# Seven block products for the down projection of a SwiGLU block, and gate and up products that stay in one PSUM bank

## The chip, the cores and the metric

The kernel runs on one core of one Trainium2 chip. The metric is the device time of one execution in microseconds (us), lower is better. One execution of the kernel before was also recorded by the hardware profiler, and all rows below come from that record.

## The reference

A transformer block in float32 on 2048 tokens of width 576: a modulated layer norm, attention with 32 heads in four segments, a residual, a second modulated layer norm, a SwiGLU feed-forward layer with 4608 hidden units, and a residual. The change is in the feed-forward layer alone:

```
x = x + ga * attention(h)                       # x: 2048 x 576
h = layernorm(x) * (1 + cb) + sb
g = silu(h @ w_gate)                            # w_gate, w_up: 576 x 4608
u = h @ w_up
x = x + gb * ((g * u) @ w_down)                 # w_down: 4608 x 576
```

## The kernel before, in words

The attention part fills the first third of the span and stays as it is, but for one transfer. The feed-forward layer then works on two halves of the tokens (`t` = 0, 1; 1024 tokens each), and in each half on 18 pairs of hidden blocks (`p`; 2 x 128 hidden units each). One pass of the inner body for one `t` and one `p` is called a step here; there are 36.

**Numbers as a high and a low part.** Every operand of a matmul is split into two reduced float32 values. For weights, ScalarE writes the high part `wh` (L1065), VectorE subtracts it and writes the low part `wl` (L1066), and GpSimd writes a small tail of `wh` (L1067). The hidden activation gets `ah` (ScalarE, L1110) and `al` (VectorE, L1111), the down weights `dh` (L1079) and `dl` (L1080). A product is high times high, low times high and high times low.

**Gate and up: seven block products.** Tokens, width and hidden units are each cut in two, which would make eight block products; the kernel makes seven (Strassen's scheme in Winograd's form) from sums of blocks. A step has 14 slots (`k`): seven products `m`, in the order `MO7`, for the gate (`z` = 0) and seven for the up weights (`z` = 1). Slot `k` runs `prod` (L1090): seven matmuls of 512 columns into one PSUM bank. The sums of weight blocks are GpSimd's (`sum_o`, L1059), those of token blocks `y` are made ahead. What the seven products mean for the four result blocks is worked out after them: VectorE adds the banks into `tx` and `ty` (L1122, L1125, L1129) and makes the four results (L1101 for the gate, which ScalarE then puts through silu at L1102; L1106 and the multiply by the gate at L1107 for the up part).

**Down: all block products.** `down` (L1152) makes, for one tile of 128 tokens, 12 matmuls of 288 columns into two banks, which VectorE adds to the running result `acc` in SBUF (L1155). Eight tiles make a step's down projection. They run one step late, at slots 4 to 11 of the next step. The down weights are loaded in `load_d`, multiplied there by `gb` on GpSimd (L1073), and split by `prep_d`. `acc` begins as the residual, so that after the last step each tile is stored as it is (L1158).

**Order.** The kernel is scheduled by hand: each engine gets its instructions in the order in which the Python code issues them, and runs them in that order. What the list `later` holds is issued at the start of the next slot. In each slot the order is: the weight split for the product seven slots ahead, the held-back subtractions, the product and its VectorE work, `sum_o`, the tile of `down`, the preparation of the down weights, and, for `t` = 0 alone, one piece of `prep2`, which makes the token blocks of the second half (`xD` to `yD`).

## Time and profile before

| | us |
|---|---|
| median of 3 runs | 1943.85 |
| lowest, highest | 1943.43, 1947.84 |
| span of the profiled execution, first to last instruction | 1946.8 |

| engine | busy us in the span | share |
|---|---|---|
| PE (TensorE matmuls) | 1901.2 | 98% |
| DVE (VectorE) | 1533.1 | 79% |
| POOL (GpSimd) | 1020.6 | 52% |
| ACT (ScalarE) | 824.8 | 42% |

The record gives the span and not the time outside it; the span is 2.9 us above the median of the runs and inside their scatter. The shares are averages over the attention and the feed-forward part. A busy PE is not the same as a PE that could not be faster, but where it is busy without a gap, and nothing waits ahead of it, the count of matmuls and the time of one set the pace.

### The profile page before, as it was taken

Reading aid. Unit: us, or ns where it says so; the run is one execution under the profiler, and the core shown is the slowest. Engines: PE = TensorE matmul, PEld = TensorE weight load, DVE = VectorE, ACT = ScalarE, POOL = GpSimd, SP = SyncE. Lnnn points to the kernel's source line nnn. Section 1 sums busy time; section 2 is a strip of 40 time slices with the busy share of each in tenths; the row PEclk is TensorE's granted clock in tenths of the full one; section 3 lists DMA queues with packets and bytes.
Section 4 is the critical chain, followed back from the end, with each engine's and each line's share of the span. In section 5 each row is a group of like instructions: output and inputs, shape, how many; then the busy total and the mean of one; then the engine's idle time right before and its main releaser. Section 6 shows DMA issues by size and latency. Waiting matters only on the chain.

```text
span 1946.8 us, 31901 instructions
## 1 busy us (share of the span) xinstructions
PE 1901.2 (98%) x11119; PEld 1593.1 (82%) x11119; DVE 1533.1 (79%) x3218; ACT 824.8 (42%) x1652; POOL 1020.6 (52%) x1396
## 2 busy tenths in 40 slices
PE   7999999999999899999999999999999999999999
PEld 4887865676766678888888888888888888888888
DVE  6575257878786999898898988979888888878886
ACT  2222256767667434344344343433333333333332
POOL 5322235455544866556565565556565564655551
PEclk9999999999999899999999999999999999999999
DMA  7776564444443332232222222174211211112111
GB/s 207 244 227 233 203 204 140 131 139 150 136 128 125 92 135 101 89 106 80 80 106 83 82 84 78 60 264 146 74 62 45 74 62 59 60 62 74 62 57 50
DMA packets 114354, 223.59 MB, mean 115 GB/s; under 512 B 22992, under 2 KB 40784, under 8 KB 112720
## 3 DMA queue, kind: packets, MB, share of 16 engines
q1 hardware_dynamic: 111936, 215.61, 34.2%
q0 software_dynamic: 576, 5.11, 0.7%
q8 instruction: 88, 1.44, 0.3%
q10 hardware_dynamic: 1680, 0.82, 0.2%
q14 instruction: 74, 0.61, 0.1%
HBM read 161.11 MB, written 60.36 MB: 114 GB/s over the span
## 4 chain that ended last, share of the span: by engine, by line
PE 88%; DVE 4%; DMA 4%; ACT 1%; issue 1%; POOL 1%; SPq 1%; POOLq 0%; ACTq 0%; DVEq 0%
PE M L1090 39%; PE pd L1152 23%; PE pp L93 4%; PE s L576 4%; PE av L596 4%; PE s L174 4%; PE pv L93 3%; PE pw L694 2%; DMA O<-in_wgu_dram 1%; DMA mD<-mr 1%; PE pn L765 1%; PE pm L429 1%; PE px L617 1%; PE pr L346 1%; DVE y L923 1%
## 5 line engine op out<-in xcount | busy, mean ns | idle before, releaser
L1090 PE MATMUL M<-y,wh 128*128 128x512 f32 x2520 | 792.0, 393 | 5.0 <-DVE cu L1106 2.1
L1090 PEld LDWEIGHTS M<-y,wh 128*128 128x128 f32 x2520 | 473.7, 188 | 101.7 <-issue 3.9
L1067 POOL TENSOR_TENSOR wh<-O,wh 32x128 fp32r<-32x128 f32 x504 | 296.6, 593 | 423.0 <-ACT wh L1065 271.3
L1090 PE MATMUL M<-y,wl 128*128 128x512 f32 x1008 | 394.7, 392 | 0.0
L1059 POOL TENSOR_TENSOR O<-O 128x384 f32<-128x384 f32 x288 | 315.4, 1095 | 75.0 <-DMA O<-in_wgu_dram 42.9
L1152 PE MATMUL pd<-dh,ah 128*128 128x288 f32 x1152 | 340.3, 295 | 0.2 <-DVE acc L1155 0.2
L1152 PE MATMUL pd<-dl,ah 128*128 128x288 f32 x1152 | 340.3, 295 | 0.0
L1152 PE MATMUL pd<-dh,al 128*128 128x288 f32 x1152 | 340.1, 295 | 0.0
L1110 ACT CAST ah<-sg 128x512 fp32r<-128x512 f32 x144 | 89.5, 621 | 547.8 <-DVE sg L1107 422.0
L1155 DVE TENSOR_TENSOR acc<-acc,pd 128x576 f32<-128x576 f32 x288 | 216.5, 752 | 111.8 <-PE pd L1152 108.4
L1066 DVE TENSOR_TENSOR wl<-O,wh 128x256 fp32r<-128x256 f32 x504 | 286.2, 568 | 6.0 <-ACT wh L1065 5.2
L179 DVE CUSTOM_DVE_ANT_0 junk<-s,tri 128x256 bf16<-128x256 f32 (+3 forms) x512 | 228.7, 487 | 77.2 <-PE s L174 69.8
L1065 ACT CAST wh<-O 128x384 fp32r<-128x384 f32 x504 | 242.8, 507 | 0.0
L1152 PEld LDWEIGHTS pd<-dl,ah 128*128 128x128 f32 x1152 | 217.4, 189 | 11.8
L1152 PEld LDWEIGHTS pd<-dh,ah 128*128 128x128 f32 x1152 | 216.7, 188 | 11.6 <-DVE acc L1155 0.6
L579 ACT ACTIVATE Pt<-s 128x512 f32<-128x512 f32 (+1 forms) x352 | 186.5, 559 | 88.1 <-PE s L576 72.0
L1152 PEld LDWEIGHTS pd<-dh,al 128*128 128x128 f32 x1152 | 216.6, 188 | 0.0
L1090 PEld LDWEIGHTS M<-y,wl 128*128 128x128 f32 x1008 | 190.0, 188 | 29.6
L1102 ACT ACTIVATE sg<-sg 128x512 f32<-128x512 f32 x144 | 91.2, 633 | 222.7 <-DVE sg L1101 222.7
L576 PE MATMUL s<-qs,ks 110*128 110x512 f32 (+2 forms) x384 | 150.5, 409 | 5.7 <-DMA qs<-mD 4.4
L174 PE MATMUL s<-ks,qs 108*128 108x256 f32 (+3 forms) x512 | 141.2, 327 | 3.3 <-DMA ks<-kD 1.4
L583 POOL TENSOR_SCALAR_AFFINE_SELECT Pt<-Pt 128x512 f32<-128x512 f32 x128 | 81.6, 648 | 100.6 <-ACT Pt L579 100.2
(428 smaller groups left out, 2836.6 us busy)
## 6 DMA issues: line engine op xcount, KB each, us to landing
O<-in_wgu_dram SPq DMA_DIRECT2D x72, 768.0 KB
ks<-kD SPq DMA_DIRECT2D x68, 216.0 KB
qs<-qD SPq DMA_DIRECT2D x68, 216.0 KB
kD<-fh SPq DMA_DIRECT2D x16, 512.0 KB
qD<-fh SPq DMA_DIRECT2D x16, 512.0 KB
yD<-st SPq DMA_DIRECT2D x28, 256.0 KB
y<-yD SPq DMA_DIRECT2D x7, 1024.0 KB
wml<-in_w_mod_dram SPq DMA_DIRECT2D x24, 216.0 KB
```

Source lines behind the costliest of these rows:

```text
L93: nc.tensor.matmul(ps, lhsT=a, rhs=b, start=(k == 0), stop=(k == 13))
L174: nc.tensor.matmul(bank[:, n * (h - h0):n * (h - h0) + n], lhsT=qst[b][0:108, h, 128 * i:128 * i + 128], rhs=kst[b][0:108, h // 2, 0:n], s ...
L179: nc.vector.tensor_tensor_reduce(junk[:, :n], bank[:, n * (h - h0):n * (h - h0) + n], tri[:, L - n:], 1.0, -3e38, op0=ALU.add, op1=ALU.max ...
L576: nc.tensor.matmul(bank[:, n * (g - h):n * (g - h + w)].rearrange("p (a b) -> p a b", a=w), lhsT=kst[u % NB][0:110, g // 2, 128 * j:128 * ...
L579: nc.scalar.activation(pt[:, h:h + per, :n], bank[:, :n * per].rearrange("p (a b) -> p a b", a=per), AF.Exp, scale=SCALE)
L1059: nc.gpsimd.tensor_tensor(o[:, d], o[:, a], o[:, b], op=op)
L1065: nc.scalar.copy(wh, o)
L1066: later.append(lambda: nc.vector.tensor_tensor(wl, o[:, 0:2], f32(wh[:, 0:2]), op=ALU.subtract))
L1067: later.append(lambda: nc.gpsimd.tensor_tensor(wh[32:64, 2], o[32:64, 2], f32(wh[32:64, 2]), op=ALU.subtract))
L1090: nc.tensor.matmul(bank, lhsT=a, rhs=b, start=(n == 0), stop=(n == 6))
L1152: nc.tensor.matmul(pd[:, h, :288], lhsT=a[:, tk], rhs=w[:, f, sl], start=(k == 0), stop=(k == 5))
L1155: nc.vector.tensor_tensor(o, o, pd[:, :, :288], op=ALU.add)
```

## The change

It does two things.

First, the down projection becomes seven block products too, with seven accumulators `acc[1]` to `acc[7]` in SBUF, each of 512 tokens by 288 columns. A block product of a step is two pieces ("chunks") of six matmuls of 288 columns. A piece is again two PSUM banks, which VectorE adds to its accumulator. So a step has 14 pieces with 84 matmuls, where it had 8 tiles with 96. The products need sums of blocks of the hidden activation, which GpSimd makes in place (`sum_a`, four per step), and of the down weights (`sum_d`, four per step). Each of the seven activation blocks and of the seven weight blocks is split into a high and a low part. The seven accumulators are put together once per half (`comb`): for the first half within the first step of the second, with two additions on GpSimd and six on VectorE, and for the second half after the last step, on VectorE alone.

Second, the gate and up products are ordered so that `m` = 1, 6, 7 and 4 add up in one PSUM bank (A), and 5 and 3 in another (C). ScalarE copies the partial sums that are needed on the way (`ta`, `tb`, `tc`), and each of the four results takes one addition at most.

With these go smaller edits: weights are split five slots ahead and not seven (`PF`, `WR`), the loads of the weights and `sum_o` move to other slots, the down weights have one buffer, the staging tile `st` of `prep2` one instead of two, a store of the attention part is issued by ScalarE instead of GpSimd, and less scratch is set aside for DMA.

In the diff, `MO7` is the order of the gate and up products and `POS` that of the down products. `CH` says how many pieces of the down projection stand in each of the 14 slots, `KS` in which slots the four `sum_a` stand, and `KA` which down product gets its `ah` in which slot.

```
+    def sum_d(p, j):
+        r = RW[p]
+        d, a, b = ((4, 1, 0), (5, 3, 4), (6, 3, 1), (7, 2, 5))[j]
+        nc.gpsimd.tensor_tensor(r[:, d], r[:, a], r[:, b], op=ALU.subtract)
+
+    def prep_d(p, m):
+        r = RW[p][:, WSLOT[m]]
+        ...
+        nc.scalar.copy(dh, r)
+        later.append(lambda: nc.vector.tensor_tensor(dl, r, f32(dh), op=ALU.subtract))
...
-    def prod(z, m):
-        bank = ps.tile([P, L], F32, tag="M", name=f"M{m}", bufs=4)
+    def prod(z, m, bank, first, last):
...
-            nc.tensor.matmul(bank, lhsT=a, rhs=b, start=(n == 0), stop=(n == 6))
+            nc.tensor.matmul(bank, lhsT=a, rhs=b, start=(first and n == 0), stop=(n == 6),
+                             skip_group_check=not first)
...
+    def step(z, m):
+        if m == 1:
+            B["A"] = ps.tile([P, L], F32, tag="A", name="A", bufs=2)
+        elif m == 2:
+            B["B"] = ps.tile([P, L], F32, tag="B", name="B", bufs=1)
+        elif m == 5:
+            B["C"] = ps.tile([P, L], F32, tag="C", name="C", bufs=1)
+        bank = B["B" if m == 2 else "C" if m in (5, 3) else "A"]
+        prod(z, m, bank, m in (1, 2, 5), m in (2, 4, 3))
+        if m == 1:
+            copy_t("ta", bank)
+        elif m == 2:
+            fin(z, (0, 0), bank, T["ta"])
+        elif m == 6:
+            copy_t("tb", bank)
+        elif m == 7:
+            copy_t("tc", bank)
+            fin(z, (1, 1), B["C"], T["tc"])
+        elif m == 4:
+            fin(z, (1, 0), bank)
+        elif m == 3:
+            fin(z, (0, 1), bank, T["tb"])
+
+    def sum_a(j):
+        d, a, b, op = (((1, 1), (0, 1), (1, 1), ALU.add), ((0, 1), (0, 0), (0, 1), ALU.subtract),
+                       ((0, 0), (1, 1), (0, 0), ALU.subtract), ((1, 0), (1, 0), (0, 0), ALU.subtract))[j]
+        nc.gpsimd.tensor_tensor(PA[d], PA[a], PA[b], op=op)
...
+    def down(t, p, c):
+        m, c = POS[c // 2], c % 2
...
+        for i in range(2):
+            tk = slice(128 * (2 * c + i), 128 * (2 * c + i) + 128)
+            for k, (a, w) in enumerate(((ah, dh), (ah, dl), (al, dh))):
+                nc.tensor.matmul(pd[:, i, :288], lhsT=a[:, tk], rhs=w, start=(k == 0), stop=(k == 2))
+        o = acc[m][:, 2 * c:2 * c + 2]
...
+            nc.vector.tensor_tensor(o, o, pd[:, :, :288], op=ALU.add)
...
+    MO7 = (1, 2, 6, 5, 7, 4, 3)
+    POS = [1, 2, 4, 5, 6, 7, 3]
+CH = (1, 1, 1, 1, 2, 1, 0, 1, 1, 1, 1, 2, 1, 0)
+KS = (0, 1, 2, 3)
+KA = ((5, 2), (6, 4), (7, 6), (3, 8))
...
                     step(z, m)
...
+                    if not last and 6 <= k < 10:
+                        sum_o(nx, 0, k - 6)
+                    if not last and k >= 11:
+                        sum_o(nx, 1, k - 11)
+                    if k == 4 and n > 14:
+                        sum_o(p, 1, 3)
...
+                            if k == KS[j]:
+                                sum_a(j)
...
+                        for _ in range(CH[k]):
+                            down(*prev, chunk)
...
+                    if k == 2:
+                        load_d(p)
+                    if k in (4, 5):
+                        mul_d(p, k - 4)
+                    if 6 <= k < 10:
+                        sum_d(p, (0, 1, 3, 2)[k - 6])
+                    if k >= 7:
+                        prep_d(p, POS[k - 7])
+                    for ij, kk, j in (((0, 0), 9, 1), ((1, 1), 12, 4), ((1, 0), 13, 2)):
+                        if k == kk:
+                            prep_a(p % 2, j, AC[ij])
```

More of the change, by code (lines that the diff above doesn't have):

```diff
@@ L1160, in block @@
+            ad(acc[4], acc[7])
+            store(t, 1, 0, acc[4], c)
+            ad(x11[t], acc[7])
+            store(t, 1, 1, x11[t], c)
+        elif m == 3:
+            ad(acc[3], acc[5])
+            store(t, 0, 1, acc[3], c)
     with tc.manual_schedule():
@@ L1248, in block @@
             sum_o(0, 1, j)
+        new_acc()
+        seq = [(t, p, z, m) for t in range(2) for p in range(NPR) for z in range(2) for m in MO7]
         prev = None
+        n = 0
         for t in range(2):
@@ L1255, in block @@
                     run(g2)
-                if not last:
-                    load_o(nx, 0)
+                    load_x11(0)
+                if last:
+                    load_x11(1)
+                chunk = 0
                 for k in range(14):
@@ L1269, in block @@
                         load_y(ACT_OP[m])
-                    if k == 7 and not last:
+                    if not last and k == 7 - PF:
+                        load_o(nx, 0)
+                    if not last and k == 14 - PF:
                         load_o(nx, 1)
-                    if not last and k % 7 in (3, 4, 5, 6):
-                        sum_o(nx, k // 7, k % 7 - 3)
-                    if prev is not None and DS <= k < DS + 8:
-                        down(*prev, k - DS)
-                    if k in DP:
-                        prep_d(p, DP.index(k))
```

207 lines of the change are left out of this document (115 added, 92 removed).

## The prediction, made before the changed kernel was run

> **What bounds the kernel now.** I read the page's busy times first, then the stretches of steady work, the chain of waits at its end, the groups by line, and the timelines of VectorE and GpSimd.
>
> ```profile
> span 1946.8 us, 31901 instructions
> PE 1901.2 (98%) x11119; PEld 1593.1 (82%) x11119; DVE 1533.1 (79%) x3218; ACT 824.8 (42%) x1652; POOL 1020.6 (52%) x1396
> ```
>
> The average hides the stages. The start of a step is the ScalarE copy of the gate's first product (L1118): first the starts that delimit the stages, then busy time in two stretches (first token half, second token half) and in one step. The columns are PE, PEld, DVE, ACT, POOL, granted clock, DMA.
>
> ```profile
> 692.83 0.58 ACT L1118 COPY tx<-M 128x512 f32<-128x512 f32 x1
> ...
> 1263.46 0.57 ACT L1118 COPY tx<-M 128x512 f32<-128x512 f32 x1
> ...
> 1335.79 0.58 ACT L1118 COPY tx<-M 128x512 f32<-128x512 f32 x1
> 692.84:1262.50 569.66, 569.04 (x3147) 503.81 (x3148) 499.96 (x801) 227.11 (x469) 338.75 (x413) 1.00 0.27 87
> 1334.80:1893.50 558.70, 558.70 (x3081) 494.96 (x3080) 454.84 (x730) 206.18 (x414) 317.38 (x382) 1.00 0.19 65
> 1680.00:1715.28 35.28, 35.28 (x196) 31.24 (x195) 29.28 (x47) 12.88 (x27) 20.04 (x24) 1.00 0.19 62
> ```
>
> PE has no gap at full clock. A step is 35.28 us in the second half and (1263.46 - 692.83) / 16 = 35.66 us in the first, where `prep2` runs beside it. Per step (stretch / 35.28 and / 35.66) VectorE is busy 28.7 us in the second half and 31.3 in the first, GpSimd 20.0 and 21.2: `prep2` costs 2.6 and 1.2. The end of the chain gives the two prices of PE.
>
> ```profile
> 1931.66 1.60 PE M L1090 x7
> 1933.26 9.57 PE pd L1152 x72
> 1942.84 0.03 issue
> 1942.86 0.76 DVE acc L1155
> ```
>
> A gate or up product costs 1.60 us, a down matmul 9.57 / 72 = 0.133. A step is 14 x 1.60 + 96 x 0.133 = 35.2, the measured one. So PE bounds the layer, and VectorE has 6.6 us to spare in a step. The last addition ends at 1943.6 and the store at 1946.8: 3.2 us.
>
> **What PE gains.** 12 down matmuls fewer are 12 x 0.133 = 1.6 us a step: 33.7 us. Over 34 full steps that would be 54 us. Whether they arrive depends on VectorE and GpSimd, which get the work.
>
> ```profile
> 1715.22 0.76 DVE L1155 TENSOR_TENSOR acc<-acc,pd 128x576 f32<-128x576 f32 x1 [0.18 <-PE pd L1152]
> 1715.89 0.42 DVE L1066 TENSOR_TENSOR wl<-O,wh 128x256 fp32r<-128x256 f32 x1
> 1716.23 0.69 DVE L1111 TENSOR_TENSOR al<-sg,ah 128x512 fp32r<-128x512 f32 x1
> 1716.83 0.69 DVE L1129 TENSOR_TENSOR tx<-M,tx 128x512 f32<-128x512 f32 x1
> 1717.43 0.68 DVE L1106 TENSOR_TENSOR cu<-M,ty 128x512 f32<-128x512 f32 x1
> 1718.15 0.72 DVE L1107 TENSOR_TENSOR sg<-cu,sg 128x512 f32<-128x512 f32 x1
> 1718.79 0.41 DVE L1066 TENSOR_TENSOR wl<-O,wh 128x256 fp32r<-128x256 f32 x1
> ```
>
> Starts tell what an instruction costs a full queue: the next independent one starts about 0.08 us before it ends. So `acc` 0.67, `wl` 0.34, `al` 0.60, an addition 0.60, `cu` with its dependent multiply 0.72 + 0.64.
>
> **VectorE's ledger, per step.** Gone: six additions into `tx` and `ty`, one gate and one up addition (the fourth result is read from PSUM): 7 x 0.60 + 0.72 = 4.9. Added: `acc` 14 times instead of 8, 6 x 0.67 = 4.0; `al` 7 instead of 4, 1.8; `dl` seven small instead of two large. A `dl` of 288 columns, by the line through `wl` (256, 0.42) and `al` (512, 0.69), takes 0.45, in a queue 0.37; the two of 576 cost 0.67 each: 2.6 - 1.3 = 1.3. From 28.7 this makes 30.9 us of 33.7, before lock waits.
>
> **GpSimd's ledger.** Groups by line, then each one's shortest, median and longest.
>
> ```profile
> L1059 POOL TENSOR_TENSOR O<-O 128x384 f32<-128x384 f32 x61 | 66.0, 1083 | 9.3 <-DMA O<-in_wgu_dram 3.3 <-DVE ty L1125 1.9
> L1067 POOL TENSOR_TENSOR wh<-O,wh 32x128 fp32r<-32x128 f32 x106 | 63.7, 606 | 113.1 <-ACT wh L1065 69.9 <-DVE wl L1066 25.3 <-PE M L1090 14.4
> L1066 DVE TENSOR_TENSOR wl<-O,wh 128x256 fp32r<-128x256 f32 x109 | 58.0, 532 | 1.3 <-ACT wh L1065 1.3
> L1065 ACT CAST wh<-O 128x384 fp32r<-128x384 f32 x109 | 52.3, 507 | 0.0
> L1066 DVE TENSOR_TENSOR wl<-O,wh x109: 407/419/1144, 1600.5 to 1869.9; 128x256 fp32r<-128x256 f32 x109
> L1059 POOL TENSOR_TENSOR O<-O x61: 1008/1017/1473, 1601.9 to 1867.6; 128x384 f32<-128x384 f32 x61
> L1067 POOL TENSOR_TENSOR wh<-O,wh x106: 449/521/977, 1600.9 to 1866.5; 32x128 fp32r<-32x128 f32 x106
> L1073 POOL TENSOR_TENSOR dr__19002<-dr__19002,gbB x1: 1432/1432/1432, 1621.7 to 1621.7; 128x576 f32<-128x576 f32 x1
> ```
>
> Undisturbed, 384 columns cost 1.02 us and 576 cost 1.43, 2.15 ns a column: a `sum_d` (288) is 0.81, a `sum_a` (512) 1.29. Eight `sum_o` 8.1, 14 tails 6.3, two multiplies 2.9 (17.3 before), four `sum_a` 5.2 and four `sum_d` 3.2: 25.7 us in 32 instructions.
>
> **The lock.** `wl` takes 407 ns at least, 532 on average and 1144 at most, the tail 449 to 977. One place shows why.
>
> ```profile
> 1701.51 0.76 DVE L1080 TENSOR_TENSOR dl<-dr__19776,dh 128x576 fp32r<-128x576 f32 x1 [0.23 <-ACT dh L1079]
> 1414.56 1.62 POOL L1073 TENSOR_TENSOR dr__16816<-dr__16816,gbB 128x576 f32<-128x576 f32 x1
> ...
> 1414.82 1.98 DVE L1080 TENSOR_TENSOR dl<-dr__16782,dh 128x576 fp32r<-128x576 f32 x1
> ...
> 1416.26 0.85 POOL L1067 TENSOR_TENSOR wh<-O,wh 32x128 fp32r<-32x128 f32 x1
> ```
>
> A `dl` that takes 0.76 alone takes 1.98 when it starts behind a GpSimd instruction that ends at 1416.18. Had it begun its 0.76 at 1416.04, 0.14 before that end, it would end as it did, at 1416.80. The tail after it, begun at 1416.26, took 0.85 instead of 0.45. So one waits for the other's end, less about 0.13. `acc`, with one input in PSUM, shows no such spread (0.76 in all rows here). The Trainium skill, page "SBUF — State Buffer", section "Who interferes with whom", says that a VectorE instruction with two SBUF inputs and a GpSimd instruction that reads SBUF lock each other out. By that rule, the trace agrees.
>
> Such VectorE instructions go from 24 a step (14 `wl`, 4 multiplies, 4 `al`, 2 `dl`) to 31 (14, 3, 7, 7), GpSimd's time from 17.3 to 25.7. Today `wl` loses 14 x 0.113 = 1.6 us a step, and GpSimd 14 x 0.157 + 8 x 0.066 = 2.7. VectorE's loss scales as 31/24 x 25.7/17.3 = 1.9: 1.5 more, so 32.4 of PE's 33.7. As a sum that just fits.
>
> **As a chain it doesn't.** `sum_a` needs the last product of the step before (slot 13), and stands at the head of GpSimd's queue. Behind it up to slot 8, in order: 4 `sum_a` 5.2, 8 tails 3.6, 4 `sum_o` 4.1, 2 multiplies 2.9, 3 `sum_d` 2.4; 18.1 us for 21 instructions, 1.5 for the gaps between them (about 0.07 each, an estimate from the 0.08 from 1416.18 to 1416.26), 2.7 lock waits (tails 8 x 0.157 x 1.2 = 1.5; the other 13 at 0.066 to 0.157, 1.2): 22.3. The third of these `sum_d` feeds `dh` of product 4 (ScalarE, under 0.51; 0.45 taken, with handovers 0.65), and its `dl` stands in VectorE's queue at slot 10, ahead of all that follows to the last multiply of slot 13: slot 10 1.6, slot 11 3.4, slot 12 2.0, slot 13 2.7: 9.7, and lock waits of 12 instructions, 1.5 to 2.6, since GpSimd is still behind there: 2.1. That multiply releases the next `sum_a`. Once round is 22.3 + 0.65 + 9.7 + 2.1 = 34.8 us, more than PE's 33.7. It is 34.2 with the low waits and 35.6 if GpSimd's waits are 0.8 longer. I take 34.8.
>
> **The sum**, against the span of 1946.8 and, with the same difference, the median 1943.85. The parts:
> - second half, 16 steps: 16 x (34.8 - 35.28) = -8.
> - first half, 16 steps: about half of `prep2`'s GpSimd time and 0.4 of its VectorE time lie in the chain, 0.6 + 1.0, taken as 1.5: 16 x (36.3 - 35.66) = +10. The single `st` buffer makes ScalarE wait for each store; ScalarE is busy 12.9 us a step and gets about 5 more, so nothing, or up to 0.5 a step if the copy `tc` is behind it.
> - first step of the second half, putting together: on GpSimd two additions of 1152 columns (2.15 ns each, 2.5 + 0.2), on VectorE six of about 1.27, four of them in the chain: 10; the step already has waits for the new `y` (its start to 1335.79 is a longer step), so +8.
> - the end: 14 pieces, 0.67 each, 16 half-additions of 576 columns at 0.69, four `al`, the first of them waiting for two `sum_a`: 1.5 + 2.6 + 22 on VectorE, and 3.2 for the store, 29 after the last product, where now six tiles at 1.6 and 0.8 + 3.2 are 13.6: +15. The last step itself has 14 pieces of 0.8 where it had ten tiles of 1.6, -5. Together +11 before rounding.
> - loads: `load_o` and `load_d` are issued at slot 2 and asked for two to four slots (5 to 10 us) later, at a DMA share of 0.19: nothing, at most 1 us a step. `vD` from another queue: nothing. Last step of the first half, where `prep2` is done: +1. The first step has no down projection in either kernel: nothing.
>
> Sum +22: 1966 us.
>
> **Rivals.**
> *PE stays the bound.* For: the sums fit, and the chain's lock waits could be smaller, since hand-placed slots need not collide at random. Then 33.7 (34.4 with `prep2`): -25 - 20 + 6 + 11 = -28, 1916. Against: VectorE at 96% of such a step, and GpSimd at 25.7 plus gaps and waits, about 90%.
> *Slower by the lock.* The unshared parts, each instruction less 0.13, are 21.5 us on GpSimd and 14 x 0.29 + 10 x 0.56 + 7 x 0.32 = 11.9 on VectorE: 33.4 in a step of 33.7. Both queues run in order, and VectorE's other work doesn't always stand where GpSimd holds the lock; if a tenth is lost, a step is 37 (38.5 with `prep2`): +28 + 45 + 8 + 11 = +92, 2036. It decides once VectorE's lock waits pass 5 us a step. Were whole instructions exclusive, it would be 25.7 + 15.9 = 41.6 a step, 34 x 6.4 = 218 more and 2160; the overlap of 0.13 in the rows speaks against that, 0.02 of this rival's chance. That is what the page of the Trainium skill named above would make of it ("the other fully blocks").
> *In-place sums.* Product 4 follows 7 in bank A and must wait for ScalarE's copy `tc`; two pieces, 1.6 us, cover a copy of 0.58. ScalarE's queue holds nothing long there, but a silu ahead waits for VectorE. 0.5 us a step on top of the sum: 1982.
>
> **Chances.** Forecast 0.40 (its own range 1946 to 1992, by the chain's 34.2 and 35.6), PE bound 0.26, lock 0.24, in-place 0.10. A measurement of this kernel can tell about 0.3%, 6 us, from no change. Same: 0.07, out of the low end of the forecast. Faster 0.27, slower 0.66. The range, 1908 to 2045, reaches a little past the prices of the first two rivals, since their steps of 33.7 and 37 are uncertain by 0.3; about a tenth is left beyond each end.
>
> **What would show it.** Right: steps of the second half of 34.5 to 35.6 with gaps on PE before L1152 ended by VectorE, `dl` waiting for `dh` and that for GpSimd's `sum_d`; `wl` at 0.6 or more; about 29 us behind the last product. Wrong: PE without a gap and steps of 33.7 (the first rival), or steps over 36 with `wl` over 0.7 (the second), or PE waiting for `tc` (the third).

## The result, and the profile after

The changed kernel takes 2122.5 us (median of four runs, 2119.3 to 2124.6) against 1943.6 us for the kernel before: 1.091 times, 95% interval 1.0892 to 1.0936. The forecast was 1966 us with a range of 1908 to 2045. The direction was right; the size was not, and the time lies outside the range.

The page of the changed kernel: span, busy times, VectorE's busy tenths in 40 slices, and the chain that ended last, by engine.

```profile
span 2122.9 us, 31782 instructions
...
PE 1925.6 (91%) x10687; PEld 1559.4 (73%) x10687; DVE 1879.0 (89%) x3456; ACT 1004.5 (47%) x2084; POOL 1385.5 (65%) x1682
...
DVE  6564278787868999999999999999999999999998
...
DVE 53%; PE 31%; issue 6%; DMA 4%; ACT 3%; POOL 3%; SPq 0%; POOLq 0%; DVEq 0%; ACTq 0%
```

PE was the bound before, at 98%. Now VectorE's row is nearly all nines from the first third of the span on, and the chain lies on VectorE for 53%.

A step begins with the ScalarE copy of the gate's first product, which is `ta` now (L1134). These starts, from the timeline of ScalarE, delimit 16 steps of the first half and 16 of the second.

```profile
689.35 0.58 ACT L1134 COPY ta<-A 128x512 f32<-128x512 f32 x1 [1.24 <-PE A L1106]
...
1351.08 0.57 ACT L1134 COPY ta<-A 128x512 f32<-128x512 f32 x1
...
1437.37 0.58 ACT L1134 COPY ta<-A 128x512 f32<-128x512 f32 x1
...
2056.88 0.59 ACT L1134 COPY ta<-A 128x512 f32<-128x512 f32 x1 [1.38 <-PE A L1106]
```

So a step is (1351.08 - 689.35) / 16 = 41.36 us in the first half, and (2056.88 - 1437.37) / 16 = 38.72 in the second. The other starts that the stages need are, in the kernel before, those of the first step of the second half and of the last step, and in the changed kernel that of the first step of the second half:

```profile
1297.45 0.58 ACT L1118 COPY tx<-M 128x512 f32<-128x512 f32 x1
...
1899.06 0.58 ACT L1118 COPY tx<-M 128x512 f32<-128x512 f32 x1
```

```profile
1387.82 0.59 ACT L1134 COPY ta<-A 128x512 f32<-128x512 f32 x1 [0.47 <-PE A L1106]
```

By stages, from these starts:

| stage | before, us | after, us | difference | forecast |
|---|---|---|---|---|
| up to the first full step | 692.8 | 689.4 | -3.5 | 0 |
| 16 steps, first half | 570.6 | 661.7 | +91.1 | +10 |
| last step of the first half | 34.0 | 36.7 | +2.7 | +1 |
| first step of the second half | 38.3 | 49.6 | +11.2 | +8 |
| 16 steps, second half | 563.3 | 619.5 | +56.2 | -8 |
| last step and end | 47.7 | 66.0 | +18.3 | +11 |
| span | 1946.8 | 2122.9 | +176.1 | +22 |

Busy time in a stretch of each half (columns: PE, PEld, DVE, ACT, POOL, granted clock, DMA share, GB/s):

```profile
690.00:1350.00 660.00, 588.62 (x2974) 495.91 (x2972) 645.85 (x900) 306.21 (x659) 504.18 (x542) 0.96 0.22 75
1500.00:1880.00 380.00, 350.13 (x1795) 293.60 (x1794) 377.90 (x515) 176.08 (x371) 293.03 (x315) 0.99 0.17 58
```

VectorE is busy for 377.9 of 380 us in the second half, 38.5 us of a step of 38.72, and for 645.85 of 660 in the first. PE has gaps and GpSimd too. What VectorE spends that time on stands in the groups by line of this second stretch (busy us and mean ns, then the idle time before them with what ended it):

```profile
L1071 DVE TENSOR_TENSOR wl<-O,wh 128x256 fp32r<-128x256 f32 x138 | 108.1, 783 | 0.0
L1210 DVE TENSOR_TENSOR acc<-acc,pd 128x576 f32<-128x576 f32 x139 | 101.3, 740 | 0.0
L1205 PE MATMUL pd<-dh,ah 128*128 128x288 f32 x276 | 87.2, 316 | 29.9 <-DVE acc L1210 29.4
L1064 POOL TENSOR_TENSOR O<-O 128x384 f32<-128x384 f32 x78 | 86.8, 1113 | 14.0 <-DMA O<-in_wgu_dram 7.3 <-DVE al L1165 1.4
...
L1165 DVE TENSOR_TENSOR al<-sg,ah 128x512 fp32r<-128x512 f32 x69 | 63.8, 925 | 1.1
...
L1171 POOL TENSOR_TENSOR sg<-sg 128x512 f32<-128x512 f32 x40 | 55.6, 1391 | 45.9 <-DVE sg L1129 39.2 <-PE pd L1205 4.4
...
L1129 DVE TENSOR_TENSOR sg<-cu,sg 128x512 f32<-128x512 f32 x30 | 28.6, 952 | 1.0
...
L1096 DVE TENSOR_TENSOR dl<-dr__19782,dh 128x288 fp32r<-128x288 f32 x7 | 6.5, 922 | 0.0
```

The instruction with an input in PSUM (`acc`) takes what it took before. Every one with two inputs in SBUF has become much longer: `wl` 783 ns where 0.41 us is the undisturbed time, `dl` 922 where it is 0.45 (as the prediction worked out, and in the last step, where GpSimd is done), `al` 925 where it is 0.68, the multiply 952 where it is 0.69. Per step that is 14 x 0.37 + 7 x 0.47 + 7 x 0.245 + 3 x 0.26 = 5.2 + 3.3 + 1.7 + 0.8 = 11.0 us of waiting. In the kernel before the same sum is 2.5 us (of it 14 x 0.13 for `wl`). Without its waits VectorE would need 38.5 - 11.0 = 27.5 us of PE's 33.7: 6.2 us of waiting had room, and 11.0 came.

Two timelines of one place show what each wait is. VectorE:

```profile
1600.03 0.80 DVE L1071 TENSOR_TENSOR wl<-O,wh 128x256 fp32r<-128x256 f32 x1
...
1601.41 1.39 DVE L1071 TENSOR_TENSOR wl<-O,wh 128x256 fp32r<-128x256 f32 x1
1602.72 0.94 DVE L1165 TENSOR_TENSOR al<-sg,ah 128x512 fp32r<-128x512 f32 x1
...
1606.66 1.48 DVE L1071 TENSOR_TENSOR wl<-O,wh 128x256 fp32r<-128x256 f32 x1
```

GpSimd at the same time:

```profile
1599.23 1.30 POOL L1171 TENSOR_TENSOR sg<-sg 128x512 f32<-128x512 f32 x1
...
1601.22 1.30 POOL L1171 TENSOR_TENSOR sg<-sg 128x512 f32<-128x512 f32 x1
1602.59 0.52 POOL L1072 TENSOR_TENSOR wh<-O,wh 32x128 fp32r<-32x128 f32 x1
...
1606.42 1.44 POOL L1082 TENSOR_TENSOR dr__18182<-dr__18182,gbB 128x576 f32<-128x576 f32 x1 [1.89 <-DMA dr__18182<-in_wd_dram]
```

The first `sum_a` ends at 1600.53; 0.13 before that, plus 0.42 for a `wl`, gives 1600.82, and the `wl` ends at 1600.83. The second ends at 1602.52 and gives 1602.81; the `wl` ends at 1602.80. The tail ends at 1603.11 and gives 1603.66 for the `al`: 1603.66. The multiply ends at 1607.86 and gives 1608.15: the `wl` ends at 1608.14. So the price of one meeting is what the prediction read from the one place in the trace of before.

I did that sum for every two-input instruction of about ten steps of the second half: each one that is more than 60 ns too long ends, to within 60 ns, as a GpSimd instruction's end less 0.13 demands. Counted so, 6 of 24 such VectorE instructions met a running GpSimd instruction per step before, 0.40 us each; after the change 23 of 31, 0.49 us each. The waits went from 2.4 to 11.2 us a step mainly because three quarters of them now meet one, where a quarter did. Per step, by the GpSimd instruction that was met:

| met | before | after |
|---|---|---|
| `sum_o`, 8 in both | 1.2 us, 2.3 meetings | 3.8 us, 7.0 meetings |
| tails, 14 in both | 0.7, 2.7 | 2.1, 7.9 |
| multiplies, 2 in both | 0.5, 1.0 | 1.4, 2.0 |
| `sum_a`, 4 new | | 2.9, 4.0 |
| `sum_d`, 4 new | | 1.0, 2.0 |

The new sums account for 3.9 of the 8.8 us directly. The other 4.9 are old instructions that used to pass between VectorE's and no longer do.

### The profile page after: what moved, and what is told of

The parts are those of the page before. It is cut to its first block, busy times and chain, and to the rows that moved or that the text cites. A ratio compares the mean times of both kernels' runs of the same rounds, so it can differ in the third digit from the quotient of the medians.

```text
span 2122.9 us, 31782 instructions
## 1 busy us (share of the span) xinstructions
PE 1925.6 (91%) x10687; PEld 1559.4 (73%) x10687; DVE 1879.0 (89%) x3456; ACT 1004.5 (47%) x2084; POOL 1385.5 (65%) x1682
## 4 chain that ended last, share of the span: by engine, by line
DVE 53%; PE 31%; issue 6%; DMA 4%; ACT 3%; POOL 3%; SPq 0%; POOLq 0%; DVEq 0%; ACTq 0%
DVE acc L1210 13%; DVE wl L1071 11%; DVE al L1165 8%; DVE dl L1096 7%; PE s L582 4%; PE pp L99 4%; PE av L602 4%; PE s L180 4%; PE A L1106 3%; DVE cu L1128 3%; DVE sg L1129 3%; DVE sg L1120 2%; PE pd L1205 2%; PE pw L700 2%; PE pv L99 2%
## 5 line engine op out<-in xcount | busy, mean ns | idle before, releaser
L1106 PE MATMUL A<-y,wh 128*128 128x512 f32 (+1 forms) x1440 | 486.9, 404 | 9.9 <-ACT tc L1134 6.0
L1071 DVE TENSOR_TENSOR wl<-O,wh 128x256 fp32r<-128x256 f32 x504 | 386.6, 767 | 2.6 <-ACT wh L1070 2.0
L1210 DVE TENSOR_TENSOR acc<-acc,pd 128x576 f32<-128x576 f32 x488 | 356.1, 741 | 0.8 <-PE pd L1205 0.5
L1106 PEld LDWEIGHTS A<-y,wh 128*128 128x128 f32 (+1 forms) x1440 | 279.3, 194 | 68.7 <-ACT tc L1134 7.4
L1171 POOL TENSOR_TENSOR sg<-sg 128x512 f32<-128x512 f32 x144 | 199.4, 1384 | 147.0 <-DVE sg L1129 120.5
L1165 DVE TENSOR_TENSOR al<-sg,ah 128x512 fp32r<-128x512 f32 x252 | 250.6, 994 | 9.2 <-ACT ah L1164 5.7
L1106 PE MATMUL C<-y,wh 128*128 128x512 f32 (+1 forms) x720 | 243.8, 404 | 0.0
L1106 PE MATMUL A<-y,wl 128*128 128x512 f32 x576 | 231.7, 402 | 0.0
L1164 ACT CAST ah<-sg 128x512 fp32r<-128x512 f32 x252 | 155.0, 615 | 136.2 <-DVE sg L1129 99.4
L1106 PEld LDWEIGHTS C<-y,wh 128*128 128x128 f32 (+1 forms) x720 | 139.9, 194 | 26.3
```

Source lines behind the costliest of these rows:

```text
L1071: later.append(lambda: nc.vector.tensor_tensor(wl, o[:, 0:2], f32(wh[:, 0:2]), op=ALU.subtract))
L1106: nc.tensor.matmul(bank, lhsT=a, rhs=b, start=(first and n == 0), stop=(n == 6), skip_group_check=not first)
L1164: nc.scalar.copy(ah, src)
L1165: later.append(lambda: nc.vector.tensor_tensor(al, src, f32(ah), op=ALU.subtract))
L1171: nc.gpsimd.tensor_tensor(PA[d], PA[a], PA[b], op=op)
L1210: nc.vector.tensor_tensor(o, o, pd[:, :, :288], op=ALU.add)
```

## The experiments

The theory was: the lock between VectorE and GpSimd lengthens VectorE's work until VectorE is full. Its rivals were the chain through the sums that the prediction had taken, VectorE full by its own work, and the in-place sums. GpSimd's reading work and the waits are us per step of the second half; the waits are summed as above, and the reading work is the recorded time of GpSimd's instructions that read, which includes GpSimd's own waits.

| kernel | us | step, first half | step, second half | GpSimd's reading work | lock waits |
|---|---|---|---|---|---|
| before | 1944 | 35.7 | 35.2 | 19.9 | 2.4 |
| after | 2122 | 41.4 | 38.7 | 30 | 11.2 |
| after, GpSimd only writes | 1920 | 34.9 | 33.9 | 0 | 0.2 |
| after, the 8 new sums only write | 2001 | 38.0 | 34.9 | 19.4 | 5.7 |
| before, 4 reading instructions more | 1950 | 35.8 | 35.2 | 24.7 | 4.9 |
| before, 8 more | 1998 | 37.8 | 36.1 | 29.7 | 9.6 |
| after, VectorE's order alternating | 2113 | 41.6 | 38.0 | 30 | 10.7 |
| after, sums on VectorE | 2105 | 41.1 | 38.0 | 20.5 | 6.8 |
| after, tail by VectorE and ScalarE | 2172 | 43.1 | 39.5 | 24.0 | 7.4 |
| the same, its copy later | 2153 | 42.8 | 38.9 | 23.8 | 8.7 |
| the same, and `sum_d` on VectorE | 2144 | 42.5 | 38.8 | 19.6 | 8.1 |
| down half alone | 2216 | 44.1 | 41.4 | 29.6 | 8.5 |
| in-place half alone | 2001 | 37.6 | 36.5 | 19.8 | 3.9 |
| the same, other slots | 1952 | 36.0 | 35.3 | 19.8 | 3.9 |

**GpSimd only writes.** All of GpSimd's step instructions, but not those of `prep2` and `comb`, become fills of the same tiles, two or three for one, so that its time stays near 25 us a step. The weight sums, tails, multiplies and activation sums are left out of the computation.

```
-        nc.gpsimd.tensor_tensor(o[:, d], o[:, a], o[:, b], op=op)
+        fill(o[:, d], o[:, d], o[:, d, 0])
...
+    def fill(d, *extra):
+        nc.gpsimd.memset(d, 0.05)
+        for e in extra:
+            nc.gpsimd.memset(e, 0.05)
```

> The changed kernel, but in each step of the feed-forward layer every GpSimd instruction that adds, subtracts or multiplies is replaced by fills of the same tile that take about as long and only write (a row of the kernel before: 512 columns 517 ns), so sums, products and tails are left out, while every count, queue, order and wait of the other engines stays. Theory 1, the lock (VectorE waits for GpSimd wherever both read SBUF through the shared interface, 11.3 us a step now): the low parts of the weights fall from 790 to about 420 ns, VectorE needs 27.3 us a step, and the step becomes PE's 33.7; 16 steps of the second half in 540 us, the whole at 1910 to 1940. Theory 2, the chain of the prediction (sums on GpSimd, then ScalarE, then VectorE): GpSimd takes as long as before, so the step stays above 33.7, at 34 to 36. Theory 3, VectorE is slowed by something else (PSUM, transfers, the granted clock of 0.97): the low parts stay near 790 ns and the step at 38.7.

Measured: 1919.7 us. A stretch of the second half and the `wl` group in it:

```profile
1400.00:1840.00 440.00, 440.00 (x2366) 385.82 (x2365) 362.20 (x676) 232.69 (x494) 330.37 (x1065) 1.00 0.19 65
...
L1077 DVE TENSOR_TENSOR wl<-O,wh 128x256 fp32r<-128x256 f32 x182 | 76.2, 418 | 0.0
```

With GpSimd busy for 75% of the time, but writing, `wl` is back at 418 ns, VectorE at 82% and PE at 100%. A step is 33.94 us, close to the prediction's 33.7 for PE as the bound, and the lock theory's range holds. So the reading is what costs: 203 us between the two, 194 of them behind the first `ta`. VectorE's own work is 362.2 / 440 x 33.94 = 27.9 us a step, and against the 38.5 of the changed kernel the waits are 10.6, close to the 11.0 from the groups. This also answers to the Trainium skill, page "SBUF — State Buffer", section "Who interferes with whom", which restricts the lock for such instructions to a GpSimd instruction that reads SBUF; the trace agrees (0.2 us of waits beside 25 us of fills).

**Only the eight new sums write.** `sum_a` and `sum_d` alone become fills; those sums are left out of the computation.

```
-        nc.gpsimd.tensor_tensor(PA[d], PA[a], PA[b], op=op)
+        fill(PA[d], PA[d], PA[d][:, :256])
...
-        nc.gpsimd.tensor_tensor(r[:, d], r[:, a], r[:, b], op=ALU.subtract)
+        fill(r[:, d], r[:, d], r[:, d, :64])
```

> As the run with fills only, but only the eight new sums (four of the activation, four of the down weights) are fills; the weight sums, tails and multiplies stay as they are. GpSimd then reads SBUF for 17.3 us a step, as in the kernel before. If lock waits grow with GpSimd's reading time alone, as the prediction scaled them from the kernel before, they fall to 3.1 x 17.3/25.7 = 2.1 us and the step is PE's 33.7. If a full VectorE queue meets the lock at almost every instruction, they fall only as the reading time does: 11.3 x 17.3/25.7 = 7.6, VectorE 34.9, the step about 35. Theory 3: 38.7.

Measured: 2000.6 us, a step of 34.9 in the second half and 38.0 in the first.

```profile
1400.00:1840.00 440.00, 432.28 (x2301) 374.12 (x2301) 417.27 (x661) 225.31 (x480) 350.89 (x605) 1.00 0.18 62
...
L1077 DVE TENSOR_TENSOR wl<-O,wh 128x256 fp32r<-128x256 f32 x177 | 114.4, 646 | 0.0
```

GpSimd reads as long as in the kernel before, yet the waits are 5.7 us, not 2.4, and `wl` takes 646 ns. Here VectorE is 95% full. `sum_o` alone, as many and as long as before, costs 3.5 us where it cost 1.2. So GpSimd's reading time by itself does not give the waits. Neither expectation had their size (2.1 and 7.6 us lie on both sides), and the step of 35 was right in part by luck, since PE is 98% busy here as well.

**The kernel before, with more reading on GpSimd.** Eight, and in a second kernel four, subtractions on a scratch tile that nothing else uses.

```
+        def busy(n):
+            nc.gpsimd.tensor_tensor(j1[:, :n], j1[:, :n], j2[:, :n], op=ALU.subtract)
...
+                    if 1 <= k < 9 and prev is not None:
+                        busy(512 if k < 5 else 288)
```

> The kernel before with eight added GpSimd instructions a step (four of 512 and four of 288 columns, on a tile that nobody uses, in slots 1 to 8), the reading load that the change adds; the store of the attention part and the DMA scratch are as in the changed kernel to make room. PE bounds this kernel and VectorE has 6.6 us to spare. The prediction's scaling: lock waits go from 2.4 to 3.6 us a step and the low parts of the weights from 532 to about 600 ns, the time stays at 1944 +- 6. If the waits depend on GpSimd's load and not on how full VectorE's queue is, each of the 24 instructions waits 0.37 as in the changed kernel: 8.9 us, low parts at 790 ns, VectorE 34 of 35.2, the time 1944 to 1975.

> The kernel before with half of the added reading GpSimd work of the earlier run: four instructions a step (2 of 512 and 2 of 288 elements, on tiles that nothing else uses), so that GpSimd has some 25 us a step instead of 20 (before) and 29.7 (eight added). Nothing of the computation is left out. Linear theory (waits in proportion to GpSimd's load, as the prediction scaled them): 2.5 us at 20 gives 3.2 at 25 and VectorE has 29.5 of 35.2: the step stays at 35.2, the time within 5 us of 1945. Threshold theory (each two-input instruction meets a running one once GpSimd's queue is backed up): waits of 4 to 6 us a step, more than linear and less than the 9.6 of the full dose; the second half still 35.2 to 35.6, since VectorE is at 31 to 33, the first half 36 to 37; time 1948 to 1975 us.

Measured: 1997.6 us with eight and 1949.6 with four. With eight:

```profile
1400.00:1840.00 440.00, 435.91 (x2362) 378.50 (x2361) 424.29 (x562) 156.76 (x316) 356.63 (x390) 1.00 0.18 60
...
L1066 DVE TENSOR_TENSOR wl<-O,wh 128x256 fp32r<-128x256 f32 x171 | 152.5, 892 | 0.0
```

With four:

```profile
1400.00:1840.00 440.00, 440.00 (x2413) 389.05 (x2412) 383.92 (x576) 162.03 (x326) 304.53 (x349) 1.00 0.18 63
...
L1066 DVE TENSOR_TENSOR wl<-O,wh 128x256 fp32r<-128x256 f32 x176 | 124.3, 706 | 0.0
```

These keep VectorE's work as it was (a store's queue and the DMA scratch are as in the changed kernel), so they show the growth that the prediction lacked: waits of 2.4, 4.9 and 9.6 us a step at 19.9, 24.7 and 29.7 us of reading work. In proportion to the load, 29.7 would give 3.6. With four, the second expectation holds (waits of 4 to 6, 1948 to 1975 us). With eight, both missed the time: 8.9 us of waits was near, but 1975 us was the most that I allowed. The share of the two-input instructions that start behind a running GpSimd instruction goes 0.30, 0.51, 0.70, and the share of GpSimd instructions that follow the one before within 0.15 us 0.71, 0.79, 0.90. Four more cost little time, since PE stays the bound while VectorE has room (384 of 440 us); eight push VectorE to 96%, and a step takes 36.1 us, more than PE's 35.2.

**VectorE's order alternating.** In each slot the product's work comes first, then the two subtractions of the weight split, and the other held-back ones one behind each `acc`, instead of all of them in a row at the start.

```
-                    for f in todo:
+                    for f in todo[:2]:
                         f()
+                    rest = todo[2:]
...
                             down(*prev, chunk)
+                            if rest:
+                                rest.pop(0)()
```

> The changed kernel with one thing moved: in each product's slot VectorE does the gate or up pair's work first, then the weight remainder, and each held-back remainder (two SBUF inputs) comes after one accumulation (one PSUM input) instead of all of them in a row. Every instruction, its engine and its size stay. Lock theory (a remainder waits for the GpSimd instruction that it finds running, so what counts is how many find one running; an accumulation of 0.68 to 0.74 us between two of them lets GpSimd start the next one, but also uses time in which VectorE would have waited): the waits fall from 11.3 us a step to some 7 to 9, the step from 38.5 to 35 to 37, the time to 2000 to 2070 us. Theory that VectorE's waits are fixed by the load alone (GpSimd's queue is always backed up, so each of the 31 finds it busy wherever it stands): within 0.5 us of 38.5 a step, 2100 to 2135 us. Theory of a chain through the sums: later remainders delay the products, 39 or more a step, over 2130 us.

Measured: 2112.8 us, a step of 38.0.

```profile
1520.00:1860.00 340.00, 313.34 (x1638) 266.67 (x1637) 339.05 (x469) 159.19 (x343) 265.83 (x288) 0.99 0.17 58
...
L1071 DVE TENSOR_TENSOR wl<-O,wh 128x256 fp32r<-128x256 f32 x126 | 102.6, 820 | 0.0
```

The waits fall only to 10.7. My expectation of 7 to 9 missed; the second theory, that in a queue this full the load settles the waits wherever an instruction stands, holds for this one other order (within 0.5 us of 38.5, 2100 to 2135 us).

**The sums on VectorE.**

```
-        nc.gpsimd.tensor_tensor(r[:, d], r[:, a], r[:, b], op=ALU.subtract)
+        nc.vector.tensor_tensor(r[:, d], r[:, a], r[:, b], op=ALU.subtract)
...
-        nc.gpsimd.tensor_tensor(PA[d], PA[a], PA[b], op=op)
+        nc.vector.tensor_tensor(PA[d], PA[a], PA[b], op=op)
```

> The changed kernel with the eight new sums of a step (four of activations, four of weight blocks) on VectorE instead of GpSimd. GpSimd's load falls from 29.8 us a step to some 20; VectorE gains eight instructions with two SBUF inputs, 4 of 512 and 4 of 288 elements (by its own two-input rows 0.42 and 0.30 us without waits: 2.9 us). Lock theory: VectorE's unblocked work is 27.2 + 2.9 = 30.1, and 39 two-input instructions meet a GpSimd that is busy for half the step with gaps, at some 0.11 to 0.18 us each = 4 to 7 us: step 34 to 37, time 1960 to 2050 us. Theory that VectorE is full by its instructions, not by waits: 38.5 + 2.9 = 41.4 a step, some 2230 us. Theory that the sums' place in the chain counts and not the load: 38.5 or less by the shorter sums, 2090 to 2120 us.

Measured: 2104.8 us, a step of 38.0.

```profile
1520.00:1860.00 340.00, 313.68 (x1638) 265.28 (x1637) 338.05 (x541) 160.96 (x342) 183.67 (x216) 1.00 0.17 58
...
L1071 DVE TENSOR_TENSOR wl<-O,wh 128x256 fp32r<-128x256 f32 x126 | 67.8, 538 | 0.0
...
L1171 DVE TENSOR_TENSOR sg<-sg 128x512 f32<-128x512 f32 x36 | 24.9, 692 | 0.0
```

The waits fall to 6.8, inside the 4 to 7 that the lock theory gave, but its step of 34 to 37 us and its 1960 to 2050 us missed: I had priced the moved sums too low, at 2.9 us: they cost 4 x 0.69 + 4 x 0.45 = 4.6. VectorE stays full: 27.3 (38.5 less the 11.2 of waits) + 4.6 + 6.8 = 38.7 by the parts, 338.05 / 340 x 38.0 = 37.8 by the stretch. The time agrees with the third theory (2090 to 2120), but not by its reason, since VectorE has no idle time that shorter sums could have filled.

**The tail off GpSimd.** VectorE works out the 32-row tail inside `wl`, ScalarE copies it into place; two buffer counts fall by one to make room.

```
-        later.append(lambda: nc.vector.tensor_tensor(wl, o[:, 0:2], f32(wh[:, 0:2]), op=ALU.subtract))
-        later.append(lambda: nc.gpsimd.tensor_tensor(wh[32:64, 2], o[32:64, 2], f32(wh[32:64, 2]), op=ALU.subtract))
+        later.append(lambda: nc.vector.tensor_tensor(wl, o, f32(wh), op=ALU.subtract))
+        later.append(lambda: nc.scalar.copy(wh[32:64, 2], f32(wl[32:64, 2])))
```

> The changed kernel with 14 of GpSimd's instructions of a step moved off it: the 32-row tail of the weight remainder is worked out inside VectorE's instruction for it (3 blocks of 128 elements instead of 2) and copied into place by ScalarE. GpSimd's load falls from 29.8 to 21.7 us a step; VectorE's own work rises by 14 x 0.13 = 1.9 to 29.1 us; ScalarE gains 14 copies of some 0.3 us, from 18 to 22 of 38. To make room there are six weight buffers for seven and seven of the other tiles for eight. Nothing is left out of the computation. Lock theory: 31 two-input instructions at the 0.17 to 0.18 us each that the kernels with 20 us of reading GpSimd work showed are 5.5 us, so VectorE has 34.6 us a step and TensorE 33.9: a step of 34.6 to 36 in the second half, some 2 more in the first, time 1990 to 2035 us. Theory that VectorE is full by its own work whatever GpSimd does: 38.5 + 1.9 = 40.4 a step, over 2140 us. Theory that GpSimd's queue counts only through the buffers it holds back: within 10 us of 2112 either way.

Measured: 2172.5 us, 1.117 times the kernel before (1.1148 to 1.1192), so slower than the changed kernel. The lock theory's 1990 to 2035 us missed. The time is in the range of the second theory (over 2140), but its step is 39.5 us and not 40.4, and VectorE is not full:

```profile
1500.00:1900.00 400.00, 364.13 (x1842) 298.94 (x1841) 370.46 (x530) 234.50 (x530) 231.20 (x181) 1.00 0.17 57
```

The waits of a 400 us stretch of the second half name a new stop: ScalarE, in order, behind VectorE's `wl` (us in total, times, longest).

```profile
ACT wh L1072 <- DVE wl L1071: 146.9, 101, 3.3
```

The next kernel puts that copy one product later, behind the product's bank copy:

```
-        later.append(lambda: nc.scalar.copy(wh[32:64, 2], f32(wl[32:64, 2])))
+        later.append(lambda: tails.append(lambda: nc.scalar.copy(wh[32:64, 2], f32(wl[32:64, 2]))))
...
                     step(z, m)
+                    for f in late:
+                        f()
```

> The kernel with the tail of the weight remainder on VectorE and ScalarE, with one thing moved: ScalarE's copy of the tail stands a product later, behind that product's bank copy, so that ScalarE does not stop for VectorE's remainder (it stood 147 us in 400 waiting for it in the run before). Lock theory: with ScalarE free again the step is VectorE's own 29.1 us and the lock, 31 x 0.18 to 0.25 us = 5.6 to 7.8 at a GpSimd load of some 22 to 24 us, so 34.7 to 37 in the second half, some 2 more in the first, 2000 to 2060 us. Theory that VectorE's own work and not the lock sets the step: 38.5 + 1.9 = 40.4, over 2140 us. Theory that the tail's place in ScalarE's queue was not the cause of the run before: within 15 us of its 2172 us.

Measured: 2153.0 us. A stretch of the second half, and the same wait in it:

```profile
1500.00:1900.00 400.00, 365.30 (x1886) 306.22 (x1885) 390.04 (x539) 239.39 (x535) 236.01 (x185) 1.00 0.16 55
...
ACT wh L1076 <- DVE wl L1075: 17.6, 23, 1.4
```

ScalarE's stop is gone, and the step goes from 39.5 to 38.9, yet the lock theory as I had put it (34.7 to 37) missed. So did the step of the theory of own work alone (40.4; its "over 2140 us" holds), and the third theory by a little (19.5 us from the run before, where it allowed 15). VectorE is 98% busy: its own 29.1 us and 8.7 us of waits. With the 14 tails gone GpSimd's recorded work fell from 30 to 23.8 us, and the waits by 2.5 us, hardly more than the 2.1 that the tails had caused. What the two buffers cost that these kernels have less was not tested. The instructions that remain on GpSimd are the long ones, and they are met as often as before (`sum_o` 7.4 of 8, 4.2 us). With `sum_d` moved to VectorE as well:

> As the kernel with the late tail copy, and the four sums of the weight blocks on VectorE as well: GpSimd falls by 4 x 1.06 = 4.3 us a step, VectorE's own work rises by 4 x 0.45 = 1.8 to 30.9, and two-input instructions become 35. Lock theory: at a GpSimd load of 17 to 18 us the wait is 0.11 to 0.17 us for each of 35, 3.9 to 6, so 34.8 to 37 a step, within 20 us of the kernel with the late tail alone: work moved to VectorE costs about what the lock gives back. Theory that load on GpSimd hardly counts: 1.8 us a step more than the kernel with the late tail alone, some 60 us.

Measured: 2143.8 us, a step of 38.8, inside the 20 us that the lock theory gave as the difference of the two, but at none of its absolute values: waits of 8.1 and 1.8 of new work. So three ways of dividing the work anew (the sums on VectorE, and the last two) ended between 38.0 and 39 us a step.

**The down half alone.** The seven-product down projection with the old sums of the gate and up banks through SBUF.

```
+        bank = ps.tile([P, L], F32, tag="M", name=f"M{m}", bufs=4)
+        prod(z, m, bank, True, True)
...
+            nc.vector.tensor_tensor(T[0], bank, T[0], op=ALU.add)
```

> The changed kernel with the gate and up products combined as before (seven products each in a bank of its own, the sums of them through SBUF on VectorE): the down projection's half of the change alone. Against the changed kernel VectorE has six more two-operand instructions a step with one PSUM and one SBUF input and ScalarE six copies fewer. TensorE has no in-place wait. Lock theory: VectorE's 27.2 unblocked gains 4 x 0.70 or so, and the waits stay at 11 or grow: step 41 to 44, time 2190 to 2320 us, so the down half costs all of the 176 us and the in-place half gives VectorE time back that it needs here. Theory that the two halves' costs add up (57 for the in-place half by its own run): 2122 - 57 = 2065 us.

Measured: 2215.7 us, a step of 41.4. The lock theory's 2190 to 2320 holds it, in part by luck, since the waits were to stay at 11 or grow and are 8.5, while VectorE's own work is larger than I put it; additive halves (2065) miss.

```profile
1560.00:1930.00 370.00, 327.37 (x1636) 274.48 (x1635) 362.95 (x540) 140.64 (x306) 262.95 (x287) 0.96 0.16 53
```

VectorE's own work, busy time less waits, is 32.1 us a step here and 27.3 in the changed kernel: the in-place half saves it 4.8 us, where the prediction's ledger had 4.9.

**The in-place half alone**, with the old down projection.

```
-            nc.tensor.matmul(bank, lhsT=a, rhs=b, start=(n == 0), stop=(n == 6))
+            nc.tensor.matmul(bank, lhsT=a, rhs=b, start=(first and n == 0), stop=(n == 6),
+                             skip_group_check=not first)
```

> One part alone: gate and up products added up in PSUM as in the changed kernel, the down projection as before (with 6 instead of 4 buffers for its activation parts, and the DMA scratch of the changed kernel). It takes 4.9 us of additions a step off VectorE and leaves PE's matmuls as they are. Theory 1 and 2: PE bounds it at 35.2 us a step, the time is 1935 to 1946; the first half may come to 35.3 a step from 35.66, which would be 6 us less. If in-place sums make PE wait for ScalarE's copies (the third rival of the prediction), 0.5 us a step or more: 1960 or above.

Measured: 2001.1 us, 1.030 times the kernel before (1.0282 to 1.0317). That is the third rival's case (1960 or above); the first theories' 1935 to 1946 missed. The groups of PE in a stretch of 440 us:

```profile
L1089 PE MATMUL A<-y,wh 128*128 128x512 f32 (+1 forms) x484 | 159.6, 395 | 11.0 <-ACT ta L1121 11.0
...
L1089 PEld LDWEIGHTS A<-y,wh 128*128 128x128 f32 (+1 forms) x485 | 91.1, 188 | 33.4 <-ACT ta L1121 16.1
```

In these 12 steps PE waits 11.0 us for the copy `ta`, and its weight loads 16.1 (much of it the same time): product 6 goes into the bank of product 1 and must not begin before ScalarE, in its order, has copied product 1 out. Between them stands product 2, but among the gate's products no tile of the down projection does, since the tiles begin at slot 4. In the changed kernel pieces stand there. So the eight tiles were given other slots:

```
-DS = 4
+TS = (1, 3, 4, 6, 8, 9, 10, 11)
...
-                    if prev is not None and DS <= k < DS + 8:
-                        down(*prev, k - DS, PA)
+                    if prev is not None and k in TS:
+                        down(*prev, TS.index(k), PA)
```

> The kernel with only the gate and up half of the change, the eight tiles of the old down projection moved to the products 1, 3, 4, 6, 8, 9, 10 and 11, so that TensorE has a tile to do after each product whose bank is added to by a later product only once a copy has read it. Theory that the 57 us which that half cost stand in TensorE waiting for the bank between a product's copy and the next product into the same bank (1.2 us a step in its trace, and shortened overlap around it): these waits go, the step falls from 36.5 to 35.2 in the second half, the time to 1935 to 1950 us, as the kernel before or just under it. Theory that it is VectorE's and GpSimd's lock or the lost order of the pieces: within 10 us of the 2001 us measured for the half without the cover.

Measured: 1952.5 us, 1.0038 times the kernel before (1.0023 to 1.0053).

```profile
L1089 PE MATMUL A<-y,wh 128*128 128x512 f32 (+1 forms) x502 | 164.1, 392 | 0.0
```

The wait is gone and the step is 35.25. 49 of the 57 us come back, a little short of the expected 1935 to 1950. PE's work is that of the kernel before, so more was not to be had; the rest lies in the first half (+5 us) and at the end (+3).

No kernel that makes the whole computation beats the kernel before.

## Why the prediction was wrong, point by point

- **PE bounds the kernel, and would need 33.7 us a step with fewer matmuls.** Right: 33.94 with the lock away. The gain was there to be had; it went into a new bound.
- **VectorE's ledger**, 30.9 us with the waits of today in it, so 28.4 without. Nearly right: 27.9 with GpSimd writing only. Its 4.9 us saved by in-place sums came out as 4.8 in the down half alone.
- **GpSimd's ledger**, 25.7 us and lock waits. Nearly right: 30 us, of which 3.7 are waits (each instruction's time over the shortest of its kind, 16 steps). Its `sum_d` took at least 0.99 us and not 0.81.
- **The price of one meeting**: the other's end less 0.13. Right, for each wait that I could pair.
- **The scaling of the lock. This is the step that failed:** "VectorE's loss scales as 31/24 x 25.7/17.3 = 1.9: 1.5 more". It took `wl`'s loss alone, and it took the chance of a meeting to grow with GpSimd's time. With the 2.5 us of all groups it gives some 4 to 5 us of waits; 11.2 were measured, and VectorE's "32.4 of PE's 33.7" came out as 38.5. The lock waits in the chain, 2.1 us for 12 instructions, rest on the same old counts. In the trace of before, 6 of 24 two-input instructions met a GpSimd instruction, although one was running 57% of the time; with VectorE full, 23 of 31 did. The kernel before with GpSimd loaded shows the curve without the change: 2.4, 4.9, 9.6.
- **The chain of 34.8 us**, the forecast. It is not what sets the step. GpSimd does wait for the last multiply before `sum_a` (39.2 of 380 us in its row), but the other end of the chain never holds: VectorE is full, `dl` waits for nothing before it starts (0.0 idle in its row), and its own length is the wait. The 33.94 of the kernel that only writes neither supports nor excludes it, since without its lock waits it is 34.8 - 2.7 - 2.1 = 30.0; what excludes it as the bound is that VectorE has no idle time.
- **"Slower by the lock", the second rival.** The right mechanism, with the right turning point ("once VectorE's lock waits pass 5 us a step"), given 0.24; its sign, steps over 36 with `wl` over 0.7, is what came (38.7, 0.78). Its size was short: 37 and 38.5 us a step were 38.7 and 41.4. It lost a tenth of the 33.4 us that had to be shared in turn; the measured loss is 16%. Its other form, whole instructions exclusive, 41.6 a step and 2160 us, was nearer the result than the forecast, and was given 0.02; it is near by luck, since the 0.13 stands in every pair that I summed, and VectorE's time is its own work and waits, not all of GpSimd's added to its own.
- **`prep2`** was to cost 1.5 us a step in the first half. It costs 41.36 - 38.72 = 2.6, its whole VectorE time, as it must where VectorE is full.
- **In-place sums**, 0.5 us a step: too much for the changed kernel, where the page has 6.0 us of waits for `tc` in the whole span. Alone, this half cost 57 us, but by `ta`, which the prediction did not look at.
- **The seams**, +8 and +11: +11.2 and +18.3. In the kernel that only writes they are +5.2 and +15.5, so at the end 4.5 us were missing from the sum whatever the lock did; the remaining 2.8 there and 6.0 at the first step of the second half go with GpSimd's reading, by the same comparison.
- **The first rival's 1916** agrees with the 1919.7 of the kernel that only writes, in part by luck: by stages that kernel gains 12.3 and 20.3 us in the two halves (predicted 20 and 25), and its attention part, which nobody touched, ended 14.5 us earlier than in the trace of before.

What stays open is the law for a full queue. The waits come in runs: in 16 steps of the changed kernel all 125 two-input instructions that stand right behind one that has waited wait too, and 67 of the 117 right behind one that hasn't; in the kernel before it is 16 of 20 and 27 of 123. So there one wait goes with the next, which a count of separate meetings cannot scale. With the eight sums only writing it does not: the two shares are 0.29 and 0.27. Why is not shown. The waits per us of GpSimd time are 0.52 for `sum_a`, 0.43 for `sum_o` and 0.25 for tails and `sum_d` in the changed kernel. That would fit short instructions passing behind an `acc` of 0.74, which shows no such wait, where long ones cannot; no run separated length from place.

## What to carry to other kernels

Before moving work to a second engine, ask whether the two exclude each other, and count the meetings in the trace as well as the price of one: here a quarter of the instructions met before and three quarters after, and a loss scaled from the old count was less than half of the new one. A cheap test is to load the old kernel's second engine with idle work of the kind to be added, which showed 9.6 us of waits with VectorE's work as it was. And a saving on the bound engine is only worth what the next engine has to spare after its waits, not by its list of instructions.

## What the runs showed of the hardware

- A GpSimd fill does not hold VectorE's two-input instructions up: 0.2 us of waits a step beside 25 us of fills, against 11.2 beside 30 us of reading work.
- The lock's cost grows faster than the load: 2.4, 4.9 and 9.6 us a step at 19.9, 24.7 and 29.7 us of GpSimd reading, with VectorE's work unchanged (GpSimd's own waits are in these times).
- In the changed kernel's first half the granted clock was 0.96, with PE busy for 588.62 of 660 us, where the kernel before had 1.00 with no gap. VectorE was busy for 645.85 us of it, so it and not PE was full there. I did not test why the clock fell, nor what it costs.
